# FFN steps behind relu and square in every slot, and result products spread over two slots, in a squared-relu attention and conv-gated FFN kernel

## The chip, the cores and the metric

The kernel runs on one core of a Trainium2 chip. The metric is device time in microseconds (us), the median of several executions. Five engines work side by side, each strictly in the order in which its instructions were written: PE (TensorE, products), DVE (VectorE), ACT (ScalarE), POOL (GpSimd) and SP, which here only issues DMAs. They wait for each other by semaphores.

## The reference

```
scores = (z @ z.T) / S                       # per batch, S = 3136, d_qk = 64
attn   = maximum(scores, 0) ** 2
x      = u * (attn @ v)                      # d_model = 256

h    = maximum(x @ w_in, 0)                  # d_ff = 1024
conv = sum_k conv_w[k] * h shifted by k - 1  # 3 taps along the sequence
out  = (h * sigmoid(conv)) @ w_out
```

There are 4 batches and everything is float32.

## The kernel before

**Tiles.** The sequence is cut into 7 blocks of 448 queries for each batch: 28 blocks, and q is the place of a block in its batch (0 to 6). For one block the keys are 25 tiles of 128 (the last one has 64). One block times one key tile is a *slot*, so there are 700 slots, and the main loop (L582) walks over k, the slot's number. Each float32 operand is held as a high half and a low half, and a product of two of them is three products on PE.

**Attention in a slot.** A *score slot* has two score products (L252, L253) that write a PSUM tile `s`, of which there are two. ACT makes `t`, its relu (L303), DVE multiplies `s` by `t`, the square (L308, `s<-s,t`), ACT copies the high half `ah` (L315), and DVE subtracts for the low half `al` (L121, `al<-s,ah`). Then PE does six products into the block's two sums (L336 to L338, `av`; four at the last tile, L340 and L341). Since the scores are symmetric, a *transposed slot* takes its relu from an earlier block: POOL splits `t` into words (L269), SP sends them to DRAM and fetches them transposed (L281, L289), POOL joins them (L295), and ACT squares them twice, into `s` (L300) and into `ah` (L313). Such a slot has no score products and no L303 and L308, but it still uses a tile `s`, and DVE still makes `al`. Of 25 slots 0, 3, 7, 10, 14, 17, 21 are transposed for q = 0 to 6. With T for a transposed slot and a point for a score slot:

```
q=3  T.T..T.T..T.T..T.T..T.T..
q=4  TT.T.T.TT.T.T.T.TT.T.T.T.
q=5  TTT.TT.TT.TT.TT.TT.TT.TT.
q=6  TTTTTT.TTTTT.TTTTT.TTTTT.
```

**The software pipeline.** In slot k the loop writes the two halves for k+2, relu and square for k+3, the products into `av` for k and the scores for k+4. So the low half `al` of k+2 has to be done before the scores of k+4 can reuse its tile `s`, in the same slot.

**The FFN.** The FFN of a block runs during the next block, in eight parts f of 128 channels. Part f starts in slot s = `FS[f]` of that block (2, 5, 8, 11, 15, 18, 21, 24). Its steps, with the slot in which each stands before the change:

- s: six products into `ph` (`ffn_in`, L369 to L371); there are two tiles `ph`, so part f+2 reuses that of f
- s+1: relu (ACT, L392, `hb`) and first tap (ACT, L401, into `ph`)
- s+2: two more taps (DVE, L406, twice)
- s+3: sigmoid (ACT, L413)
- s+4: gate (DVE, L420); where the running block has q of 0 to 2 it writes a tile `c`, so that `ph` is free then; where q is 3 to 6 it stays in `ph`
- s+5: high half `gh` (ACT, L124); for q of 0 to 2 the low half `gl` on POOL as well
- s+6: for q of 3 to 6 the low half `gl` on DVE (L121, `gl<-ph,gh`), and only then is `ph` free
- s+9: three result products for each of the two halves of the output (`ffn_out`, L437 to L439)

After the last part the result is copied out of PSUM (`evac`, ACT, L459, s+10) and stored (L466, s+12). `gate_x` (L345) and `split_x` (L354) make the FFN's input at the end of a block.

**What sets the order.** The schedule is written by hand. `at(slot, class, function)` puts a step into a list, and in every slot the loop issues: class 0 (PRE), then the halves for k+2, class 1 (MID), relu and square for k+3, class 2 (VEC), class 3 (POST), the transposed tiles' steps, class 4 (PE0), the `av` products and scores, and class 5 (PE1). The constants L34 to L38 give slots and classes of the FFN's steps. A list `need` (L509) sorts the 16 pieces of the FFN's weights by the slot of their first use, and `WS` (L43) gives the n-th of them its place in the first two blocks.

Of the kernel before, what the change touches and what calls it, by code (L numbers as in the profile page):

```python
# [30 lines left out]


FS = [2, 5, 8, 11, 15, 18, 21, 24]
RELU, TAP, ST1, ST2, SIG, GATE, GHI, GLO, OUT0, OUT1 = 1, 1, 2, 2, 3, 4, 5, 6, 9, 9  # L34
EVAC = 10
XS = 1

C_GATE, C_ST, C_G, C_SIG, C_HI, C_LO, C_TAP, C_XS, C_EV, C_V = 0, 1, 1, 1, 1, 0, 3, 3, 0, 5  # L38

QV = 3  # L40

# [16 lines left out]
def kernel(  # L58
# [418 lines left out]
    def at(slot, cls, fn, *args):  # L477
        ev[slot][cls].append((fn, args))


    for q in range(2, QB):
        s = (7 * q) // 2 - LA - 2
# [8 lines left out]
    for b in range(1, B):  # L491
        k0 = (b * QB - 1) * NJ
        for q in range(QB):
            s = k0 - (QB - 2 - q) * NJ + (12 if q % 2 == 0 else 4)
            if q == QB - 2:
                s = k0 + 6
            elif q == QB - 1:
                s = k0 + NJ + 6
# [3 lines left out]
        for j in range(0, NJ, 2):  # L502
            s = k0 + max(last[j] + 2, last.get(j + 1, 0) + 2, V0 + V1 * j // NJ)
# [6 lines left out]
    for i, (_, what, f) in enumerate(sorted(need)):  # L510
        s = WS[i]
# [8 lines left out]
    for blk in range(NBLK - 1):  # L520
        k0 = (blk + 1) * NJ
        at(k0, C_GATE, gate_x, blk, G)
        at(k0 + XS, C_XS, split_x, blk, (G, G))
        for f in range(FC):
            s = k0 + FS[f]
            at(s, POST, ffn_halo, blk, f)
            at(s, PE1, ffn_in, blk, f)
            at(s + RELU, C_TAP, ffn_relu, blk, f)
            at(s + TAP, C_TAP, ffn_tap, blk, f)
            at(s + ST1, C_ST, ffn_conv, blk, f, 1)  # L530
            at(s + ST2, C_ST, ffn_conv, blk, f, 2)
            at(s + SIG, C_SIG, ffn_sig, blk, f)
            lo = V if (blk + 1) % QB >= QV else G
            at(s + GATE, C_G, ffn_gate, blk, f, lo)
            at(s + GHI, C_HI, ffn_hi, blk, f, A)
            at(s + (GLO if lo is V else GHI), C_LO if lo is V else PE1, ffn_lo, blk, f, lo)
            at(s + OUT0, PE0, ffn_out, blk, f, 0)
            at(s + OUT1, PE0, ffn_out, blk, f, 1)
        at(s + EVAC, C_EV, evac, blk)
        at(s + EVAC + 2, POST, store, blk)  # L540

# [107 lines left out]
```

## Time and profile before

| what | value |
|---|---|
| median of 3 runs | 1726.66 us (1726.58 to 1726.93) |
| the profiled execution, its own time | 1727.9 us |
| its span | 1726.1 us |
| PE busy | 1629.6 us (94%), 7656 products |
| DVE busy | 1228.5 us (71%) |
| ACT busy | 1257.5 us (73%) |
| POOL busy | 985.2 us (57%) |
| mean granted clock of PE | 0.992 |
| DMA | 184.58 MB, 107 GB/s on the mean |

PE's ends are modelled, so its busy share is no measure of how near it is to its peak; the distance from one product's start to the next one's is. Start times in the views count from the span's start. In the view by windows the columns are the window, its length, PE's busy time with the number of products, the granted clock, and the DMAs. In the chain of waits they are start, length and instruction, where "issue" is time in which nothing that the profile shows was waited for. In the waits they are who waited for whom, the sum, how often and the longest.

### The profile page before, as it was taken

The numbers are of one execution on the slowest core, as the hardware profiler recorded it, in microseconds if no ns is written. First come the engines' busy times: TensorE is split into PE (matmuls) and PEld (weight loads), VectorE is DVE, ScalarE is ACT, GpSimd is POOL, SyncE is SP. The second block draws the span as 40 slices with busy tenths as digits, with TensorE's granted clock in tenths as the row PEclk, the third lists the DMA queues.
The fourth block names the chain that finished last, engine by engine and source line by source line (L and its number), as shares of the span: only waits on it lengthen the run. The fifth ranks groups of instructions, "written<-read, shape, count | busy, mean of one in ns | idle before, by whom it ended". The sixth has DMA issues, their size and how long they took to land.

```text
span 1726.1 us, 24617 instructions
## 1 busy us (share of the span) xinstructions
PE 1629.6 (94%) x7656; PEld 1429.2 (83%) x7656; DVE 1228.5 (71%) x2080; ACT 1257.5 (73%) x2562; POOL 985.2 (57%) x1345
## 2 busy tenths in 40 slices
PE   6788999999999999999999999999999999999997
PEld 4577888888888888888888888888888888888886
DVE  5788667776777667777767767777776776777766
ACT  5576677778776767778876677777877766777785
POOL 5766655556555665556565565555657555555551
PEclk9899999999999999999999999999999999999999
DMA  5543443457324334445543334454633334344540
GB/s 151 152 116 92 111 102 92 109 118 147 114 76 123 102 89 113 101 107 116 121 137 83 105 104 101 94 114 105 145 94 126 93 82 114 97 100 100 111 97 22
DMA packets 384485, 184.58 MB, mean 107 GB/s; under 512 B 275297, under 2 KB 383329, under 8 KB 384353
## 3 DMA queue, kind: packets, MB, share of 16 engines
q1 hardware_dynamic: 384208, 182.77, 42.9%
q8 instruction: 60, 0.98, 0.3%
q14 instruction: 73, 0.59, 0.1%
q10 hardware_dynamic: 144, 0.23, 0.0%
HBM read 36.59 MB, written 80.28 MB: 68 GB/s over the span
## 4 chain that ended last, share of the span: by engine, by line
PE 47%; ACT 22%; DVE 19%; issue 8%; DMA 1%; POOL 1%; SPq 0%; ACTq 0%; POOLq 0%; DVEq 0%
PE av L336 6%; DVE al L121 6%; PE av L337 6%; PE av L338 6%; ACT ah L315 5%; DVE s L308 5%; PE s L252 5%; DVE ph L406 5%; ACT ph L401 4%; PE ph L371 4%; PE ph L369 4%; ACT hb L392 4%; PE ph L370 4%; PE s L253 3%; PE o L439 3%
## 5 line engine op out<-in xcount | busy, mean ns | idle before, releaser
L121 DVE TENSOR_TENSOR al<-s,ah 128x448 fp32r<-128x448 f32 x672 | 418.2, 622 | 402.1 <-ACT ah L315 243.7
L336 PE MATMUL av<-ah,vl 128*128 128x448 f32 x1344 | 494.9, 368 | 13.6 <-POOL vl L121 8.4
L337 PE MATMUL av<-ah,vh 128*128 128x448 f32 x1344 | 494.3, 368 | 0.0
L338 PE MATMUL av<-al,vh 128*128 128x448 f32 x1344 | 493.1, 367 | 0.0
L315 ACT CAST ah<-s 128x448 fp32r<-128x448 f32 x412 | 219.5, 533 | 272.1 <-DVE s L308 271.5
L295 POOL COPY tj<-tp 128x896 uint16<-128x896 uint16 x288 | 351.5, 1225 | 0.3
L406 DVE SCALAR_TENSOR_TENSOR ph<-hb,cw,ph 128x448 f32<-128x448 f32 (+1 forms) x448 | 306.6, 685 | 12.2 <-ACT ph L401 4.4
L269 POOL COPY pl<-t 128x896 uint16<-128x896 uint16 x312 | 291.8, 943 | 16.2 <-DMA dq<-pl 13.8
L308 DVE TENSOR_TENSOR s<-s,t 128x448 f32<-128x448 f32 x412 | 258.1, 626 | 49.7 <-ACT t L303 49.4
L394 POOL COPY halo<-hb 128x2 f32<-128x2 f32 x192 | 35.8, 187 | 451.1 <-ACT hb L392 451.1
L336 PEld LDWEIGHTS av<-ah,vl 128*128 128x128 f32 x1344 | 254.3, 189 | 39.4 <-POOL vl L121 11.0
L337 PEld LDWEIGHTS av<-ah,vh 128*128 128x128 f32 x1344 | 254.3, 189 | 20.6
L338 PEld LDWEIGHTS av<-al,vh 128*128 128x128 f32 x1344 | 254.0, 189 | 20.8
L303 ACT ACTIVATE t<-s 128x448 f32<-128x448 f32 x412 | 224.4, 545 | 33.1 <-POOL pl L269 16.2
L252 PE MATMUL s<-zq,zhh 128*128 128x448 f32 x412 | 176.4, 428 | 72.9 <-DVE al L121 62.6
L252 PEld LDWEIGHTS s<-zq,zhh 128*128 128x128 f32 x412 | 78.4, 190 | 155.3 <-DVE al L121 140.2
L369 PE MATMUL ph<-xh,wih 128*128 128x448 f32 x448 | 165.2, 369 | 4.9 <-DVE gl L121 4.9
L413 ACT ACTIVATE ph<-ph 128x448 f32<-128x448 f32 (+1 forms) x224 | 119.7, 534 | 67.0 <-DVE ph L406 66.3
L437 PE MATMUL o<-gh,wol 128*128 128x448 f32 (+1 forms) x448 | 164.4, 367 | 0.6 <-ACT gh L124 0.6
L371 PE MATMUL ph<-xl,wih 128*128 128x448 f32 x448 | 164.8, 368 | 0.0
L370 PE MATMUL ph<-xh,wil 128*128 128x448 f32 x448 | 164.7, 368 | 0.0
L439 PE MATMUL o<-gl,woh 128*128 128x448 f32 (+1 forms) x448 | 163.9, 366 | 0.8 <-POOL gl L121 0.8
(78 smaller groups left out, 2515.9 us busy)
## 6 DMA issues: line engine op xcount, KB each, us to landing
dq<-pl SPq DMA_DIRECT2D x252, 224.0 KB, 2.4
ut<-in_u_dram SPq DMA_DIRECT2D x28, 448.0 KB, 4.1
vst<-in_v_dram SPq DMA_DIRECT2D x48, 256.0 KB, 3.0
dq<-pl SPq DMA_DIRECT2D x84, 112.0 KB, 2.4
out_dram<-ob SPq DMA_DIRECT2D x20, 448.0 KB, 3.7
zt<-in_z_dram SPq DMA_DIRECT2D x28, 224.0 KB, 3.2
tp<-dq SPq DMA_TRANSPOSE x288, 3.3
wr<-in_moe_w_in_dram SPq DMA_DIRECT2D x8, 256.0 KB, 3.5
```

Source lines behind the costliest of these rows:

```text
L121: eng.tensor_tensor(out=out, in0=a, in1=b.bitcast(F32), op=ALU.subtract)
L252: nc.tensor.matmul(s[:, :NB], lhsT=zhh[:, w], rhs=zq[blk], start=True, stop=False)
L269: nc.gpsimd.tensor_copy(pl[k], rl.pop(k).bitcast(U16).rearrange("p (n h) -> p h n", h=2))
L295: nc.gpsimd.tensor_copy(tj[k].bitcast(U16).rearrange("p (n h) -> p h n", h=2), t)
L308: nc.vector.tensor_tensor(out=s, in0=s, in1=rl[k], op=ALU.mult)
L315: nc.scalar.copy(ah[k], sc[k][:, :NB])
L336: nc.tensor.matmul(o, lhsT=vl[:, j, d], rhs=h, start=first, stop=False)
L337: nc.tensor.matmul(o, lhsT=vh[:, j, d], rhs=h, start=False, stop=False)
L338: nc.tensor.matmul(o, lhsT=vh[:, j, d], rhs=l, start=False, stop=False)
L369: nc.tensor.matmul(o, lhsT=wih[:, dc, w], rhs=xh[blk][:, dc], start=(dc == 0), stop=False)
L371: nc.tensor.matmul(o, lhsT=wih[:, dc, w], rhs=xl[blk][:, dc], start=False, stop=(dc == DC - 1))
L406: nc.vector.scalar_tensor_tensor(out=c, in0=hb[blk, f][:, k : e + k], scalar=cw[:, f, k : k + 1], in1=c, op0=ALU.mult, op1=ALU.add,)
```

## The change

Only constants change, and `C_ST` is split in two:

```diff
-RELU, TAP, ST1, ST2, SIG, GATE, GHI, GLO, OUT0, OUT1 = 1, 1, 2, 2, 3, 4, 5, 6, 9, 9
-EVAC = 10
+RELU, TAP, ST1, ST2, SIG, GATE, GHI, GLO, OUT0, OUT1 = 1, 1, 2, 2, 3, 4, 5, 6, 10, 11
+EVAC = 12
 XS = 1
 
-C_GATE, C_ST, C_G, C_SIG, C_HI, C_LO, C_TAP, C_XS, C_EV, C_V = 0, 1, 1, 1, 1, 0, 3, 3, 0, 5
+C_GATE, C_ST1, C_ST2, C_G, C_SIG, C_HI, C_LO = 0, 2, 2, 2, 3, 3, 2
+C_TAP, C_XS, C_EV, C_V = 3, 3, 3, 5
...
-            at(s + ST1, C_ST, ffn_conv, blk, f, 1)
-            at(s + ST2, C_ST, ffn_conv, blk, f, 2)
+            at(s + ST1, C_ST1, ffn_conv, blk, f, 1)
+            at(s + ST2, C_ST2, ffn_conv, blk, f, 2)
```

On DVE the taps and the gate go from between the low half and the square (class 1) to behind the square (class 2), and `gl` from the slot's start (class 0) to behind the square. On ACT the sigmoid and `gh` go from between `ah` and relu (class 1) to behind relu (class 3), and the copy `evac` from the slot's start to class 3. On PE a part's result products stood together at s+9, and now the first half stands at s+10 and the second at s+11, so that of three slots one has the `ffn_in` products, one the first and one the second half (for the parts in slots 15, 18 and 21 the first half falls into the slot of the `ffn_in` products). `evac` and the store move by two slots. POOL's `gl` stays at its place, though its input `gh` is written later in the slot. `need` sorts a little differently, so that from the fourth piece on `w_in` pieces come sooner and `w_out` pieces later, at the same places. The number of instructions is the same. The last block's own FFN has constants of its own and is not touched. In the changed kernel every line number is higher by one.

On ACT, in a block with q = 0, these are the rows of its slots 8, 9 and 10 before the change (`t` is relu, `zhh` and `vh` prepare the next batch, `gh` stands in slot 10):

```order
L315 CAST ah<-s 128x448
L413 ACTIVATE ph<-ph 128x450
L303 ACTIVATE t<-s 128x448
L315 CAST ah<-s 128x448
L303 ACTIVATE t<-s 128x448
L137 CAST zhh<-zt 128x448
L392 ACTIVATE hb<-ph 128x448
L401 ACTIVATE ph<-hb,cw 128x450
L124 CAST vh<-vst 128x512
L315 CAST ah<-s 128x448
L124 CAST gh<-c 128x450
L303 ACTIVATE t<-s 128x448
```

And these are the same three slots with the change:

```order
L316 CAST ah<-s 128x448
L304 ACTIVATE t<-s 128x448
L414 ACTIVATE ph<-ph 128x450
L316 CAST ah<-s 128x448
L304 ACTIVATE t<-s 128x448
L138 CAST zhh<-zt 128x448
L393 ACTIVATE hb<-ph 128x448
L402 ACTIVATE ph<-hb,cw 128x450
L125 CAST vh<-vst 128x512
L316 CAST ah<-s 128x448
L304 ACTIVATE t<-s 128x448
L125 CAST gh<-c 128x450
```

The sigmoid (`ph<-ph`) and `gh` have changed places with the `t` behind them. On DVE, in a block with q = 0, slots 6 to 8 before the change (`s<-s,t` is the square, L406 the taps, L420 the gate):

```order
L121 TENSOR_TENSOR al<-s,ah 128x448
L420 TENSOR_TENSOR c<-ph,hb 128x450
L308 TENSOR_TENSOR s<-s,t 128x448
L121 TENSOR_TENSOR al<-s,ah 128x448
L406 SCALAR_TENSOR_TENSOR ph<-hb,cw,ph 128x450 x2
L308 TENSOR_TENSOR s<-s,t 128x448
L121 TENSOR_TENSOR al<-s,ah 128x448
L308 TENSOR_TENSOR s<-s,t 128x448
```

With the change:

```order
L122 TENSOR_TENSOR al<-s,ah 128x448
L309 TENSOR_TENSOR s<-s,t 128x448
L421 TENSOR_TENSOR c<-ph,hb 128x450
L122 TENSOR_TENSOR al<-s,ah 128x448
L309 TENSOR_TENSOR s<-s,t 128x448
L407 SCALAR_TENSOR_TENSOR ph<-hb,cw,ph 128x450 x2
L122 TENSOR_TENSOR al<-s,ah 128x448
L309 TENSOR_TENSOR s<-s,t 128x448
```

Low half and square now follow each other, and the FFN's step comes third. On DVE, in a block with q = 3, slots 10 and 11 before the change, where slot 11 has the `ffn_in` products of a part on PE and `gl` of the part two before it on DVE:

```order
L121 TENSOR_TENSOR al<-s,ah 128x448
L406 SCALAR_TENSOR_TENSOR ph<-hb,cw,ph 128x448 x2
L308 TENSOR_TENSOR s<-s,t 128x448
L121 TENSOR_TENSOR gl<-ph,gh 128x448
L121 TENSOR_TENSOR al<-s,ah 128x448
L308 TENSOR_TENSOR s<-s,t 128x448
```

With the change:

```order
L122 TENSOR_TENSOR al<-s,ah 128x448
L309 TENSOR_TENSOR s<-s,t 128x448
L407 SCALAR_TENSOR_TENSOR ph<-hb,cw,ph 128x448 x2
L122 TENSOR_TENSOR al<-s,ah 128x448
L309 TENSOR_TENSOR s<-s,t 128x448
L122 TENSOR_TENSOR gl<-ph,gh 128x448
```

`gl`, which frees the tile `ph`, was first in its slot and is now third.

## The prediction

> **What bounds the kernel now.** First I ask how far PE is from its own pace. The timeline gives a stretch without stalls: its first and last product, with 33 steps between them, and the one behind them.
>
> ```profile
> 475.88 0.36 PE L369 MATMUL ph<-xh,wih 128*128 128x448 f32 x1
> ...
> 482.58 0.36 PE L338 MATMUL av<-al,vh 128*128 128x448 f32 x1
> 482.88 0.47 PE L252 MATMUL s<-zq,zhh 128*128 128x448 f32 x1
> ```
>
> (482.58 - 475.88) / 33 = 0.203 us for a product, and a product that had to wait comes 0.1 us later still (0.30 instead of 0.20), as its weight load isn't hidden. Next, the windows, cut at the ends of blocks 1 and 2, of blocks 7 to 13 (one batch, q = 0 to 6) and of the last batch as a whole (the one between fills 859.3 to 1275.7).
>
> ```profile
> 82.90:149.80 66.90, 58.54 (x266) 0.97 0.42 117
> 149.80:214.80 65.00, 59.84 (x279) 0.97 0.37 94
> 442.40:507.80 65.40, 62.66 (x293) 1.00 0.38 117
> 507.80:570.90 63.10, 60.93 (x289) 1.00 0.36 102
> 570.90:631.10 60.20, 58.38 (x280) 1.00 0.36 98
> 631.10:692.10 61.00, 57.38 (x276) 1.00 0.42 104
> 692.10:749.10 57.00, 55.44 (x266) 1.00 0.48 104
> 749.10:803.80 54.70, 54.26 (x261) 1.00 0.50 106
> 803.80:859.30 55.50, 54.23 (x260) 1.00 0.58 127
> 1275.70:1689.30 413.60, 401.05 (x1911) 1.00 0.41 101
> ```
>
> Length minus products times 0.203 is what PE loses. For q = 0 to 6: 5.9, 4.4, 3.4, 5.0, 3.0, 1.7, 2.7 us, together 26 of 417. The batches behind take 416.4 (859.3 to 1275.7) and 413.6 us, so this repeats. A block is thus within 3 to 9% of PE's pace, and no reordering can win more than that. Who makes PE wait, and what do ACT and DVE wait for? From the waits:
>
> ```profile
> ACT ah L315 <- DVE s L308: 271.5, 244, 3.1
> PE s L252 <- DVE al L121: 62.6, 109, 3.7
> DVE s L308 <- ACT t L303: 49.4, 115, 1.8
> PE ph L369 <- DVE gl L121: 4.9, 5, 3.7
> ```
>
> PE waits for `al`, which frees the tile `s` for the scores. ACT waits for the square far more than PE waits for anything. Why, the chain of waits shows for one part of the FFN in the block with q = 0, from its `ffn_in` products to the next part's relu:
>
> ```profile
> 451.75 0.20 PE ph L369
> ...
> 452.76 0.21 PE ph L371
> 453.00 0.55 ACT hb L392
> 453.64 0.64 ACT ph L401
> 454.28 0.36 ACT vh L124
> 454.64 0.08 issue
> 454.72 0.54 ACT ah L315
> 455.28 0.62 DVE al L121
> 455.90 0.61 DVE ph L406
> 456.57 0.56 issue
> 457.14 0.63 DVE s L308
> 457.82 0.41 issue
> 458.22 0.54 ACT ph L413
> 458.76 0.47 ACT t L303
> 459.26 0.64 DVE s L308
> 459.95 0.41 issue
> 460.35 0.55 ACT t L303
> 460.90 0.45 ACT zhh L137
> 461.35 0.46 ACT hb L392
> ```
>
> From 453.00 to 461.35 the chain never passes through PE: 8.35 us of ACT and DVE by turns (the "issue" at 457.82 is the `ah` that the square released). PE's share of three score slots is 36 products, 7.31 us. **In these blocks the ping-pong of ACT and DVE is the bound, not PE.** Three FFN steps stand in it only because of their place: the taps ahead of the square (455.90 to 457.14, 1.24 us), and the sigmoid ahead of relu (458.22 to 458.76, 0.54 us); elsewhere the gate and `evac`.
>
> **The change part by part.** *Taps and gate behind the square, sigmoid, `gh` and `evac` behind relu.* No instruction is added, so the price is only where they stand. In the new order a part's chain from its first relu (hb) runs: to `al` 453.00 to 455.28 less the 0.44 of `vh` and issue, which not every part has: 1.84 us. Then square and taps. DVE's steps without a wait follow at 0.53 us, as two rows of its timeline show:
>
> ```profile
> 652.87 0.62 DVE L121 TENSOR_TENSOR gl<-ph,gh 128x448 fp32r<-128x448 f32 x1
> 653.40 0.61 DVE L121 TENSOR_TENSOR al<-s,ah 128x448 fp32r<-128x448 f32 x1
> ```
>
> So `al` to square 0.53, square to taps 0.53, taps 1.24, the next `al` 0.62 and 0.06 until PE: 4.82 us after hb the scores of slot s+7 are free. PE reaches them 28 products and a step after its last `ffn_in` product, 29 x 0.203 = 5.89, and hb starts 0.24 after that product (452.76 to 453.00): at 5.65. If the square has to wait for PE's scores instead, these start 10 steps after the last `ffn_in` product, relu 0.44 later (0.20 for the second product and the 0.24), the square 0.57 behind it, that is 2.80 after hb in place of 2.37, and the tile is free at 5.25. Both come before 5.65, and with a `vh` (0.44) still before or beside it: **in blocks with q of 0 to 2 PE becomes the bound.** What covers the taps is the `ah` of the next slot and PE's slack of 0.4 us; without it they cost what exceeds it. I leave 0.8 us a block for `queries`, `xh`, `evac` and the 0.1 us of exposed weight loads (it lies between nothing and the 1.7 us that the best block loses now). Won: q = 0 to 2, 5.9 + 4.4 + 3.4 - 2.4 = 11.3 us in each of three batches, 33.9. Blocks 1 and 2 of the first batch lose 12.9 and 8.4 us, much of it to preparing weights, which stays; I count only what their like win later, 3.6 + 2.6 = 6.2, with 0 and 21 as ends.
>
> *`gl` behind the square, for q of 3 to 6.* Here a wait grows. The `ffn_in` products of part f+2 need `ph`, which `gl` of part f frees, in the same slot, in six of eight parts (part 2's and 3's `gl` come a slot earlier than the products). Before, `gl` ran while DVE waited for `ah` anyway, and only 5 products waited for it. Now it stands behind `al` and square. Queued behind the waiting product are the next slot's `av` products and scores, and hb on ACT. The path from one `ffn_in` to the next, all by the rows above: hb to `al` 1.84, `al` to taps 0.53, taps 1.24, `al` to `gl` 0.53, `gl` 0.62, release and exposed weight load 0.17, six products and hb 1.25 (451.75 to 453.00): 6.18 us, and 0.53 for each square that stands in it, so 6.71 with one and 7.24 with two. Against it stand the products of these three slots. For q = 3: slot 8, one square, 32 products (6.50): 0.21 short; slots 11 and 21, two squares, 34 products (6.90): 0.34 each; slot 24, one square, 27 products (5.48): 1.23. Together 2.1. In the same way q = 4 gets 0.21, 0.21, 0.70, q = 5 0.21, 1.10, q = 6 twice 0.09, 0.21, 0.95; 5.9 us a batch in all. With 0.8 us a block for the rest as above, 12.4 (now) - 5.9 - 3.2 = 3.3 us are won in each of four batches, 13.2. The ends are no such wait at all (+23.6) and the rival below.
>
> *The result products in two slots.* The same 48 a block, now 14, 11 and 11 products in three slots and not 20, 8 and 8. They are in the counts above; by itself it wins nothing where PE is the bound. Its operands are ready four slots earlier (`gl` at s+6 at the latest). `evac` now has one slot, not two, until the next block's first result product overwrites `o`: relu and two copies, three ACT steps of at most 0.64 (the rows above), against the 14 products of slot 11, 2.84 us. It costs nothing. The store and transposes on SP's queue move by a slot or two, far ahead of a use. In POOL's queue `gl` waits about 0.5 us longer for `gh`, and the words for DRAM behind it; POOL was 57% busy, so nothing, and at worst the same 0.5 us for the 88 of them in 11 blocks, were each to reach PE, 44 (in the second rival).
>
> *Weights and the two ends.* The 16 pieces keep their places, and their steps end slots ahead of use: 0, between -3 and +3 us (the lost time of blocks 1 and 2 has such steps). Block 0 has no FFN. Behind the last block one or two slots' worth of result products and `evac` come later among the 36.8 us that the span (1726.1) goes on after 1689.3, with another FFN in them: 0, between -1 and +1.5.
>
> Sum: 33.9 + 6.2 + 13.2 = 53 us, off the profiled execution's 1727.9 (span 1726.1 and 1.8 around it): 1674.6. The runs' median lies 1.2 below it: **1673 us**.
>
> [...] DVE's square waited 115 times for relu, 49.4 us, so what stands behind a square waits as well. [...] That is the third rival's mechanism; if all 49.4 us fell on PE the sum would be nearly nil.
>
> **The rivals.** *PE alone is left.* Neither `gl` nor the rest makes it wait: 53 + 23.6 + the 0.8 of some 25 blocks, half of it, 10: 1640 to 1655. For it: `gl`'s shortfalls are tenths. Against: slot 24 lacks 0.7 us or more in every one of these blocks.
>
> *The wait for `gl` is three times as dear.* Some 94 `ffn_in` groups at 0.45 us, 42 instead of 23.6 us, and stalls of POOL's queue beside it: 1690 to 1712. For it: the estimate is made of steady paths, and each stall delays hb and the chain behind it.
>
> *Slower.* One mechanism: `gl` stands behind a square that itself waits for relu, so that `ffn_in` begins only after `al`, square and `gl`: 0.53 + 0.53 + 0.62 + 0.17 less the two score products' 0.41, 1.44 us; say 1.0 us for 94 groups, 94 us in place of 23.6: 1673 + 70 = 1743. It decides from (53 + 23.6) / 94 = 0.8 us a group. [...] Against: transposed slots have no square, and they are 10 to 21 of 25 in exactly these blocks.
>
> *Nothing happens*, because ACT's waits were never PE's: 1722 to 1730. Against it stands the chain, which for 8.35 us doesn't touch PE.
>
> **How the numbers follow.** Forecast (1655 to 1695) 0.62; PE alone 0.10; dearer `gl` 0.14; slower 0.08; nothing 0.06, of which 0.04 is within 0.2% (3.5 us, about what a measurement of this kernel can tell from no change). Faster: 0.62 + 0.10 + 0.14 + 0.02 = 0.88. The range 1650 to 1706 leaves out the last two cases, a third of the first rival and a sixth of the second, 0.2 in all.
>
> **What would show it.** Right: ACT's wait for the square falls from 271.5 us to under 100; the windows with q = 0 come to 60 to 61 us; PE's wait for `al` falls by more than half; a wait of `ffn_in` for `gl` appears, 15 to 35 us, most at slot 24. Wrong: q = 0 still over 63 us (the chain then has something that I haven't seen), or windows with q of 3 to 6 longer than now (`gl`), or new waits of L252 or L437 for POOL.

## The result, and the profile after

The changed kernel takes 1699.38 us (median of 4 runs, 1699.05 to 1699.81), beside 1726.62 us of the kernel before on the same chip: ratio 0.9846, 95% interval 0.9829 to 0.9863. That is 27 us won; 53 were forecast. The time lies in the range, the direction is right, and half of the gain is missing. The profiled span went from 1726.1 to 1697.7 us at the same mean granted clock, 0.992.

From the page of the changed kernel, busy time by engine and the chain's shares (before, on the kernel's page, the chain was `PE 47%`, `ACT 22%`, `DVE 19%`):

```profile
PE 1615.3 (95%) x7656; PEld 1433.9 (84%) x7656; DVE 1215.1 (72%) x2080; ACT 1277.1 (75%) x2562; POOL 982.5 (58%) x1345
...
PE 72%; DVE 13%; issue 6%; ACT 6%; POOL 1%; DMA 1%; SPq 0%; POOLq 0%; DVEq 0%; ACTq 0%
```

The same products and about the same busy time on ACT and DVE (before 1257.5 and 1228.5 us), but the chain now runs through PE for 72% of the span. DVE's 13% is what is left to explain. The waits of the changed kernel (who waited for whom, sum in us, times, longest):

```profile
ACT ah L316 <- DVE s L309: 97.0, 215, 2.5
DVE s L309 <- ACT t L304: 77.2, 177, 2.2
PE s L253 <- DVE al L122: 31.0, 33, 2.6
PE ph L370 <- DVE gl L122: 26.0, 35, 3.1
```

ACT's wait for the square fell by 174.5 us and PE's idle time until `al` by half. The wait of `ffn_in` for `gl`, once 4.9 us in 5 places, grew to 26.0 in 35. The weight loads of the same line (PEld) show it in 59 places, the 35 among them:

```profile
PEld ph L370 <- DVE gl L122: 47.2, 59, 3.4
```

Idle times rest on modelled ends, so from here on I count *lost starts*: the distance from one product's start to the next, less 0.203 us, wherever it is over 0.24. By the line of the late product that gives, over the whole trace: before `ffn_in` 8.2 us before the change and 46.4 after it (5.9 and 5.1 of them in the last block's own FFN, which the change doesn't touch), before the scores 126.1 and 61.3, in all 160.5 and 131.0. Next, the windows of the same blocks as in the prediction, 1 and 2 and then q = 0 to 6 (window, length, PE busy with its products, granted clock, DMA share, GB/s). Each begins behind the last `av` product of the block before, so it also holds the scores and `ffn_in` of that block's slot 24:

```profile
82.90:145.70 62.80, 57.66 (x259) 0.94 0.44 119
145.70:207.00 61.30, 57.99 (x280) 1.00 0.39 105
435.60:498.10 62.50, 60.59 (x293) 1.00 0.42 127
498.10:558.20 60.10, 59.34 (x290) 1.00 0.37 104
558.20:616.00 57.80, 57.50 (x279) 1.00 0.40 105
616.00:676.80 60.80, 57.40 (x276) 1.00 0.41 103
676.80:734.90 58.10, 55.47 (x265) 1.00 0.48 102
734.90:789.40 54.50, 53.84 (x262) 1.00 0.51 108
789.40:844.40 55.00, 53.95 (x260) 1.00 0.56 124
```

Length less products times 0.203: blocks 1 and 2 lose 10.2 and 4.5 us, q = 0 to 6 lose 3.0, 1.2, 1.2, 4.8, 4.3, 1.3 and 2.2. Against the kernel before, q = 0 to 2 won 8.3 us a batch, blocks 1 and 2 won 6.6, and **q = 3 to 6, which were to win 3.3, lost 0.2**. Lost starts, put to the slot in which each product stands and added up over the whole trace, say it more sharply: 28.3 us won in q = 0 to 2, 6.8 in blocks 1 and 2, and 7.6 lost in q = 3 to 6. The largest part of the miss lies there. One of its places, at the end of slot 7 and in slot 8 of the block with q = 3 (timeline: start, length, instruction, and in brackets the idle time before it and what ended it):

```profile
637.28 0.36 PE L254 MATMUL s<-zq,zll 128*128 128x448 f32 x1
...
637.68 0.55 ACT L304 ACTIVATE t<-s 128x448 f32<-128x448 f32 x1 [0.94 <-PE s L254]
...
638.26 0.63 DVE L309 TENSOR_TENSOR s<-s,t 128x448 f32<-128x448 f32 x1 [0.39 <-ACT t L304]
...
638.50 0.37 PE L339 MATMUL av<-al,vh 128*128 128x448 f32 x1
...
638.80 0.61 DVE L122 TENSOR_TENSOR gl<-ph,gh 128x448 fp32r<-128x448 f32 x1
...
639.47 0.47 PE L370 MATMUL ph<-xh,wih 128*128 128x448 f32 x1 [0.61 <-DVE gl L122]
```

PE's last score product, relu, square, `gl`, and back to PE: 637.28 to 639.47, 2.19 us. PE had seven steps to do in it (the last score product and six of `av`), 1.42 us. `gl` had all its inputs 2.5 us before (`gh` was done at 636.27); it waited only because it is behind a square that waits for relu. The prediction's path to `ffn_in` entered only at `hb`. This second entrance isn't in it.

This place is an example, not the rule. In blocks 1 to 27, 73 groups of `ffn_in` start late, by 41.3 us together. Followed back from `gl` by what released each step, 24 of them (16.2 us) go back to PE's scores, relu and square: 8 as here (7.0 us, slot 8 with q = 3 and 4), 16 with the two taps and an `al` between that square and `gl`. 39 (21.0 us) go back to `hb` and the `ffn_in` products ahead of it, the prediction's own path; 9 (3.5 us) to an `al` that waited for products of `av`; one in block 1 (0.6 us) waited for no `gl` on DVE.

### The profile page after: what moved, and what is told of

It reads as the page before. It is cut to its first block, busy times and chain, and to the rows that moved or that the text cites. A ratio compares the mean times of both kernels' runs of the same rounds, so it can differ in the third digit from the quotient of the medians.

```text
span 1697.7 us, 24837 instructions
## 1 busy us (share of the span) xinstructions
PE 1615.3 (95%) x7656; PEld 1433.9 (84%) x7656; DVE 1215.1 (72%) x2080; ACT 1277.1 (75%) x2562; POOL 982.5 (58%) x1345
## 4 chain that ended last, share of the span: by engine, by line
PE 72%; DVE 13%; issue 6%; ACT 6%; POOL 1%; DMA 1%; SPq 0%; POOLq 0%; DVEq 0%; ACTq 0%
PE av L337 11%; PE av L338 11%; PE av L339 11%; PE ph L370 6%; PE ph L372 5%; PE ph L371 5%; PE s L253 5%; PE o L440 4%; PE o L438 4%; PE o L439 4%; PE s L254 4%; DVE al L122 3%; DVE s L309 3%; DVE ph L407 3%; ACT t L304 2%
## 5 line engine op out<-in xcount | busy, mean ns | idle before, releaser
L337 PE MATMUL av<-ah,vl 128*128 128x448 f32 x1344 | 496.0, 369 | 10.2 <-POOL vl L122 7.8
L309 DVE TENSOR_TENSOR s<-s,t 128x448 f32<-128x448 f32 x412 | 258.7, 628 | 78.2 <-ACT t L304 77.2
L338 PEld LDWEIGHTS av<-ah,vh 128*128 128x128 f32 x1344 | 254.8, 190 | 20.4
L393 ACT ACTIVATE hb<-ph 128x448 f32<-128x448 f32 x224 | 122.6, 547 | 118.8 <-PE ph L372 117.2
L253 PE MATMUL s<-zq,zhh 128*128 128x448 f32 x412 | 163.6, 397 | 39.8 <-DVE al L122 31.0
L370 PE MATMUL ph<-xh,wih 128*128 128x448 f32 x448 | 171.9, 384 | 28.1 <-DVE gl L122 26.0
L314 ACT ACTIVATE ah<-tj 128x448 fp32r<-128x448 f32 x288 | 165.1, 573 | 0.0
```

Of the source, the lines that this page charges most:

```text
L309: nc.vector.tensor_tensor(out=s, in0=s, in1=rl[k], op=ALU.mult)
L337: nc.tensor.matmul(o, lhsT=vl[:, j, d], rhs=h, start=first, stop=False)
L338: nc.tensor.matmul(o, lhsT=vh[:, j, d], rhs=h, start=False, stop=False)
L370: nc.tensor.matmul(o, lhsT=wih[:, dc, w], rhs=xh[blk][:, dc], start=(dc == 0), stop=False)
```

## The experiments

Two suspects: what `gl` inherits from the square, and the spread, which was priced at nothing although the products in question could cover exactly that path. Medians, ratios to the runs of the kernel before that stood beside each, with 95% intervals, and lost starts in us. The medians of the kernel before in these groups of runs lie between 1725.8 and 1728.6 us, so the difference of two kernels from different groups is good to about 3 us.

| kernel | us | ratio | lost before `ffn_in` | before scores | all |
|---|---|---|---|---|---|
| before | 1726.6 | 1 | 8.2 | 126.1 | 160.5 |
| the change | 1699.4 | 0.9846 (0.9829 to 0.9863) | 46.4 | 61.3 | 131.0 |
| order_only | 1674.8 | 0.9699 (0.9683 to 0.9715) | 32.9 | 51.7 | 106.0 |
| spread_only | 1726.0 | 0.9997 (0.9988 to 1.0007) | 12.0 | 114.0 | 158.6 |
| out_9_10 | 1689.4 | 0.9775 (0.9759 to 0.9792) | 40.9 | 56.7 | 120.5 |
| gl_mid | 1677.0 | 0.9714 (0.9699 to 0.9728) | 24.3 | 59.7 | 108.7 |
| gl_first | 1686.4 | 0.9759 (0.9745 to 0.9774) | 11.5 | 82.6 | 120.3 |
| gl_only | 1762.8 | 1.0212 (1.0197 to 1.0227) | 65.1 | 103.7 | 195.8 |
| taps_back | 1724.2 | 0.9981 (0.9971 to 0.9990) | 48.7 | 88.8 | 156.1 |
| ctile | 1665.0 | 0.9636 (0.9621 to 0.9650) | 5.1 | 65.7 | 97.5 |
| ctile_before | 1742.4 | 1.0093 (1.0078 to 1.0108) | 3.1 | 141.9 | 174.8 |
| ctile_together | 1649.2 | 0.9556 (0.9540 to 0.9571) | 4.3 | 51.5 | 79.7 |
| mid_together | 1659.4 | 0.9604 (0.9590 to 0.9619) | 14.1 | 54.6 | 90.9 |
| first_together | 1670.1 | 0.9665 (0.9651 to 0.9679) | 6.7 | 72.3 | 103.5 |
| ctile_9_10 | 1657.2 | 0.9595 (0.9578 to 0.9612) | 3.6 | 59.2 | 90.0 |
| ctile_10_10 | 1707.0 | 0.9887 (0.9870 to 0.9905) | 5.0 | 111.5 | 139.9 |

### The two halves of the change apart

`order_only` has the new order and keeps the result products together at s+9 (its edit stands against the changed kernel):

```diff
-RELU, TAP, ST1, ST2, SIG, GATE, GHI, GLO, OUT0, OUT1 = 1, 1, 2, 2, 3, 4, 5, 6, 10, 11
-EVAC = 12
+RELU, TAP, ST1, ST2, SIG, GATE, GHI, GLO, OUT0, OUT1 = 1, 1, 2, 2, 3, 4, 5, 6, 9, 9
+EVAC = 10
```

> The new order within a slot, but the result products together at s+9 as before. Theory 1, with the refinement that the square ahead of gl waits for scores that PE itself made one slot earlier, so that only the products between those scores and ffn_in cover gl: six result products more stand there, 1.2 us, and the wait of ffn_in for gl falls from 45 to under 15 us; 1670 to 1690 us, faster than the change. As I put it in the prediction (the spread by itself wins nothing): within 5 us of 1699. Theory 2: 1700 to 1712 us, since 20, 8 and 8 products fit the other engines worse.

`spread_only` is the kernel before with the result products spread:

```diff
-RELU, TAP, ST1, ST2, SIG, GATE, GHI, GLO, OUT0, OUT1 = 1, 1, 2, 2, 3, 4, 5, 6, 9, 9
-EVAC = 10
+RELU, TAP, ST1, ST2, SIG, GATE, GHI, GLO, OUT0, OUT1 = 1, 1, 2, 2, 3, 4, 5, 6, 10, 11
+EVAC = 12
```

> The kernel before with only the result products spread (s+10, s+11, evac at s+12); the order within a slot is the old one. By both theories the ping-pong of ACT and DVE stays the bound for q of 0 to 2 and gl stays first: 1720 to 1735 us, a difference of at most 0.5% from the kernel before.

The order alone wins 52 us; the spread on the old order changes nothing. Together they win 27, so **on the new order the spread costs 25 us**: 13 more lost before `ffn_in` (32.9 to 46.4) and 10 more before the scores (51.7 to 61.3). The latter is all in slot 24, which has no result product with the spread and six without it: it loses 16.1 us in place of 3.6, the other slots 45.2 in place of 48.2. The time of `order_only` lay in the expected range, but not for the expected reason alone: the wait at `ffn_in` was to fall under 15 us and stayed at 33. The windows of `order_only`, for the same nine blocks:

```profile
82.40:145.70 63.30, 57.36 (x266) 0.98 0.44 122
145.70:205.30 59.60, 57.42 (x280) 1.00 0.41 105
429.50:491.40 61.90, 61.12 (x294) 1.00 0.41 123
491.40:550.30 58.90, 58.84 (x290) 1.00 0.38 109
550.30:607.60 57.30, 57.18 (x280) 1.00 0.40 104
607.60:665.90 58.30, 57.19 (x276) 1.00 0.43 108
665.90:721.90 56.00, 54.81 (x266) 1.00 0.49 106
721.90:776.40 54.50, 53.89 (x262) 1.00 0.51 108
776.40:831.60 55.20, 54.35 (x260) 1.00 0.57 126
```

By the same reckoning q = 0 to 6 lose 2.2, 0.0, 0.5, 2.3, 2.0, 1.3 and 2.4 us here. With the spread it is 0.8, 1.2 and 0.7 us more in q = 0 to 2, and 2.5 and 2.3 more in q = 3 and 4. Slot 8 with q = 3, in the timeline of `order_only`:

```profile
626.71 0.36 PE L254 MATMUL s<-zq,zll 128*128 128x448 f32 x1
626.91 0.37 PE L438 MATMUL o<-gh,wol 128*128 128x448 f32 x1
...
627.58 0.62 DVE L122 TENSOR_TENSOR al<-s,ah 128x448 fp32r<-128x448 f32 x1
...
628.11 0.62 DVE L309 TENSOR_TENSOR s<-s,t 128x448 f32<-128x448 f32 x1
...
628.64 0.61 DVE L122 TENSOR_TENSOR gl<-ph,gh 128x448 fp32r<-128x448 f32 x1
...
629.14 0.36 PE L339 MATMUL av<-al,vh 128*128 128x448 f32 x1
...
629.34 0.44 PE L370 MATMUL ph<-xh,wih 128*128 128x448 f32 x1
```

From the last score product to the end of `gl` the path is even longer than in the change (626.71 to 629.25, 2.54 us; there 637.28 to 639.41, 2.13), since an `al` comes ahead of the square. But PE now has six result products to do first, 13 steps, 2.63 us, and `ffn_in` starts 0.20 us behind the last `av`. In the change these six stand at slots 9 and 10 and cover nothing here.

### How much cover

`out_9_10`, against the changed kernel, has the first half at s+9 and the second at s+10:

```diff
-RELU, TAP, ST1, ST2, SIG, GATE, GHI, GLO, OUT0, OUT1 = 1, 1, 2, 2, 3, 4, 5, 6, 10, 11
-EVAC = 12
+RELU, TAP, ST1, ST2, SIG, GATE, GHI, GLO, OUT0, OUT1 = 1, 1, 2, 2, 3, 4, 5, 6, 9, 10
+EVAC = 11
```

> The changed kernel with the result products one slot earlier (s+9 and s+10, evac at s+11), so that three of them stand between the scores that the square ahead of gl needs and the ffn_in products that wait for gl. Theory 1 (those products cover the path scores, relu, square, gl): the wait lies between that of the change (no result products there) and of order_only (six): 1682 to 1692 us, and lost starts before L370 and L371 of 36 to 43 us (45 and 32 in the other two). Theory 2 (what costs is that they are spread over two slots): within 5 us of 1699.

In the change three of the eight slots with `ffn_in` (15, 18, 21) also hold three result products, in `out_9_10` all eight hold three, in `order_only` five (2, 5, 8, 11, 24) hold six: 9, 24 and 30 products a block. The lost starts before `ffn_in` are 46.4, 40.9 and 32.9 us, and the times 1699.4, 1689.4 and 1674.8, in `out_9_10` as expected. The time moves more than this one wait, so the scores take part.

### `gl` at other places in its slot

Class 1 is between `al` and the square (`gl_mid`, whose edit of the changed kernel this is), class 0 the slot's start, as before the change (`gl_first`, with 0 in the same place).

```diff
-C_GATE, C_ST1, C_ST2, C_G, C_SIG, C_HI, C_LO = 0, 2, 2, 2, 3, 3, 2
+C_GATE, C_ST1, C_ST2, C_G, C_SIG, C_HI, C_LO = 0, 2, 2, 2, 3, 3, 1
```

> The changed kernel with gl between al and the square (class 1 in place of 2), the result products spread as in the change. If the wait of ffn_in for gl comes from the square ahead of gl, which itself waits for relu and so for PE's scores of the slot before (theory 1), it falls from 45 us of lost starts before L370 and L371 to under 15, and al is held up less than with gl ahead of it: 1665 to 1682 us. If gl is late only because it stands behind al at all (theory 2), the wait stays over 30 us and the time within 8 us of 1699.

> The changed kernel with gl back at the start of its slot, ahead of al. Theory 1: the wait for gl goes, al in these slots comes up to 0.53 us later in about 94 slots, a third of which reach PE: 1665 to 1680 us. Theory 2: 1690 us or more, the wait for al grows by what the wait for gl loses.

`gl_only` is the kernel before with this step alone of the change:

```diff
-C_GATE, C_ST, C_G, C_SIG, C_HI, C_LO, C_TAP, C_XS, C_EV, C_V = 0, 1, 1, 1, 1, 0, 3, 3, 0, 5
+C_GATE, C_ST, C_G, C_SIG, C_HI, C_LO, C_TAP, C_XS, C_EV, C_V = 0, 1, 1, 1, 1, 2, 3, 3, 0, 5
```

> The kernel before with gl alone moved behind the square (class 2), all else old: result products together at s+9, taps and gate ahead of the square. Theory 1: the six result products cover a part of the path, and the taps no longer share the slot, so 12 to 30 us more than before, 1738 to 1757 us, all of it in windows with q of 3 to 6. If gl is hidden anyway there: within 4 us of 1727.

One place earlier, ahead of the square only, halves the wait (46.4 to 24.3) and takes 22 us off the time: so about half of it is what `gl` gets from standing behind the square. That is the square's own 0.53 us on DVE as well as its wait for relu: in the change the square right ahead of `gl` had waited for relu in 8 of the 73 late groups only, those with 7.0 us. The time lies in the range of theory 1; the rest of the wait, which it put under 15 us, stays. At the slot's start the wait all but goes (11.5), but then `gl` delays `al`, and the scores lose 21 us more (61.3 to 82.6); the time came between the ranges of the two theories. Neither place is free. On the old order the step alone makes the kernel 37 us *slower* than the kernel before beside it, dearer than expected; there the square right ahead of `gl` had waited for relu in 41 of 78 late groups, with 48.0 us lost. In the waits of `gl_only`:

```profile
PE s L252 <- DVE al L121: 46.3, 87, 2.4
PE ph L369 <- DVE gl L121: 42.7, 47, 3.6
```

So this step of the change costs, and the rest pays for it.

### The taps alone ahead of the square again

The changed kernel, `taps_back` with its one edit:

```diff
-C_GATE, C_ST1, C_ST2, C_G, C_SIG, C_HI, C_LO = 0, 2, 2, 2, 3, 3, 2
+C_GATE, C_ST1, C_ST2, C_G, C_SIG, C_HI, C_LO = 0, 1, 1, 2, 3, 3, 2
```

> The changed kernel with the two taps alone put back ahead of the square. If the taps are the main part of the ping-pong of ACT and DVE (1.24 us a part in the chain of before), the windows with q of 0 to 2 lose much of what the change won there (8.3 us a batch): they get 1 to 2.5 us longer each, and with q of 3 to 6 the path to gl gets no longer where the square comes later: 1704 to 1722 us. If the sigmoid's and gate's places are what counts: within 5 us of 1699.

25 us slower than the change, a little more than expected: without the taps' new place the rest of the change is worth 2 to 4 us. 19.0 us more are lost in q = 0 to 2, 2.1 a block, as expected, and 6.4 more in q = 3 to 6, which was not. In the waits and, for the block with q = 0, on the timeline of `taps_back`:

```profile
ACT ah L316 <- DVE s L309: 181.3, 228, 2.1
...
PE s L253 <- DVE al L122: 54.2, 86, 2.6
```

```profile
441.88 0.55 ACT L304 ACTIVATE t<-s 128x448 f32<-128x448 f32 x1
441.91 0.62 DVE L122 TENSOR_TENSOR al<-s,ah 128x448 fp32r<-128x448 f32 x1 [1.71 <-ACT ah L316]
...
442.45 1.40 DVE L407 SCALAR_TENSOR_TENSOR ph<-hb,cw,ph 128x448 f32<-128x448 f32 x2
...
443.76 0.63 DVE L309 TENSOR_TENSOR s<-s,t 128x448 f32<-128x448 f32 x1
```

Relu is done at 442.43, and the square waits for the two taps until 443.76. This is the prediction's main mechanism, and it is shown: ACT's wait for the square comes back (97.0 to 181.3) and PE's for `al` with it.

### The wait for `gl` taken out: the tile `c` for every block

If the gate writes a tile `c` also for q of 3 to 6, `ph` is free at the gate and `ffn_in` doesn't wait for `gl`. `ctile` has this edit on the changed kernel, `ctile_before` the same on the kernel before.

```diff
-        if lo is nc.gpsimd:
+        if lo is nc.gpsimd or blk < NBLK - 1:
             cc[blk, f] = o = wk.tile([P, NB + 2], F32, tag="c", name="c", bufs=2)[:, :e]
```

> The changed kernel, but the gate writes a tile c in all blocks (so far only where q is 0 to 2), and gh and gl read that. So ph is free at the gate, two slots earlier, and ffn_in cannot wait for gl; gl itself stays behind the square. Theory 1 (the shortfall of the prediction is the wait of ffn_in for gl, some 45 us by the gaps between PE's products): nearly all of it comes back, 1655 to 1668 us, and the windows with q of 3 to 6 each lose less than 2 us against PE's pace. Theory 2 (in these blocks ACT and DVE are late anyway, and the wait for gl is only where it shows): PE waits for al in its place, 1685 to 1700 us.

> Control: the kernel before with the c tile in all blocks. gl was first in its slot, and only 5 products waited for it (4.9 us), so the tile by itself is worth little by either theory: 1718 to 1729 us. If the tile wins much more than that, ctile's gain is not that of the wait for gl.

The wait is gone (46.4 to 5.1) and the time falls by 34 us to 1665.0, within the expected range. (The blocks with q = 4 were to lose under 2 us and lose 3.1 by lost starts, half of it before the scores of slot 18.) On the kernel before the same edit was to win a little or nothing and *cost* 16 us. There `gl` stands at the slot's start, ahead of `al`, and it takes longer itself (838 ns on the mean, not 616; more on that at the end); the scores lose 142 us in place of 126. That the delay of `al` is the way from the one to the other is argued, not isolated.

### What the spread still costs without that wait

`ctile_together` is `ctile` with the edit below; `ctile_9_10` has 9, 10 and 11 there, `ctile_10_10` 10, 10 and 11.

```diff
-RELU, TAP, ST1, ST2, SIG, GATE, GHI, GLO, OUT0, OUT1 = 1, 1, 2, 2, 3, 4, 5, 6, 10, 11
-EVAC = 12
+RELU, TAP, ST1, ST2, SIG, GATE, GHI, GLO, OUT0, OUT1 = 1, 1, 2, 2, 3, 4, 5, 6, 9, 9
+EVAC = 10
```

> The new order in a slot, the c tile in all blocks, and the result products together at s+9. With ffn_in free of gl, theory 1 says that the spread neither costs nor wins much (the block losses for q of 0 to 2 add up to 3.4 us a batch together and 4.0 spread): 1655 to 1668 us, within 6 us of ctile (1665). If the spread itself costs, whatever gl does (theory 2): 1640 to 1650 us.

> ctile (no wait for gl) with the result products one slot earlier, at s+9 and s+10, still spread. Theory A (what the spread costs beside gl is that no result product stands in slots 23 and 24, where PE comes early to the scores and waits for al; ctile loses 11 us in slot 24 of blocks 7 to 26, ctile_together 1.5): slot 24 now has three, so its loss falls to 3 to 7 us and the time to 1653 to 1660 us. Theory B (20, 8 and 8 suits ACT and DVE better than 14, 11, 11, wherever they stand): 1662 to 1668 us.

> ctile with all six result products of a part together, but at s+10, so again none in slots 23 and 24. Theory A: the loss in slot 24 stays near 11 us, 1660 to 1670 us. Theory B (together is better than spread): 1645 to 1655 us.

With the wait for `gl` gone, the products together at s+9 still win 16 us (1665.0 to 1649.2): the theory that the spread harms only through `gl` is refuted. `ctile_together` is the fastest kernel here, 77 us ahead of the kernel before and 50 ahead of the change; its waits and its chain:

```profile
PE s L253 <- DVE al L122: 21.5, 36, 2.6
```

```profile
PE 78%; ACT 9%; DVE 5%; issue 3%; POOL 3%; DMA 1%; SPq 0%; POOLq 0%; ACTq 0%; DVEq 0%
```

Is it being together, or the place? `ctile_10_10` has them together one slot later and is 58 us slower than `ctile_together`, outside both theories' ranges. So it is the place. In blocks 7 to 26 the scores lose 17.0 us with the products at 9 and 9, 20.4 at 9 and 10, 27.3 at 10 and 11, and 63.7 at 10 and 10. By their places, most of the eight parts have in that order 6, 3, 3 and 0 of these products on PE in slot s+2, where the taps are behind the square, or at the start of s+3, ahead of the scores that wait for the `al` behind those taps. Apart from slot 24 they lose 15.6, 12.8, 16.1 and 49.3 us: with none of these products much is lost, and three are as good as six. This is worked out from the order and was not isolated. Between 9 and 9, 9 and 10, and 10 and 11 the difference is mostly slot 24's. One of the two theories had put the whole gain on slot 24, which has four `av` products in place of six: there `ctile` loses 11.2 of its 27.3 us, `ctile_9_10`, with three result products in that slot, 7.6 (its time is as that theory had it), and `ctile_together`, with six, 1.5. `ctile_10_10`, which loses 12.5 and 10.1 us at slots 2 and 11 as well as 14.4 at slot 24, shows that it isn't the whole.

`mid_together` and `first_together` are `gl_mid` and `gl_first` with the edit of `order_only`.

> The new order, result products together at s+9, and gl between al and the square; no c tile, so gl keeps an operand in PSUM. Theory 1: both remedies add up, the wait for gl all but goes (lost starts before L370 and L371 under 8 us): 1640 to 1655 us, no slower than ctile_together (1649). If gl ahead of the square holds up the square, and so al of the next slot, more than it saves: 1660 to 1675 us.

> The new order, result products together, gl first in its slot as in the kernel before: all of the change that concerns taps, gate, sigmoid, gh and evac, and nothing else. Theory 1: al comes 0.53 us later in some slots, as in gl_first (1686 spread), less the 16 to 25 us that the spread costs: 1655 to 1672 us.

1659.4 and 1670.1: `mid_together` lies between its two ranges, with 14.1 us still lost before `ffn_in`, `first_together` in its own. Against `gl_mid` and `gl_first` the place of the result products is worth 18 and 16 us. With three ways to treat `gl` it is thus 16 to 18 us, and 25 where `gl` is behind the square.

## Why the prediction was half right

The measured gains beside the forecast's terms (us), once by the windows, each batch's figure times three or four as there, and once by lost starts, each put to its own slot and added up over the whole trace:

| term | forecast | order_only, windows | the change, windows | order_only, lost starts | the change, lost starts |
|---|---|---|---|---|---|
| q = 0 to 2 | 33.9 | 33.0 | 24.9 | 34.9 | 28.3 |
| q = 3 to 6 | 13.2 | 17.6 | -0.8 | 9.1 | -7.6 |
| blocks 1 and 2 | 6.2 | 9.2 | 6.6 | 10.1 | 6.8 |
| block 0 and the end | 0 | | | 0.5 | 2.0 |
| sum | 53.3 | 59.8 | 30.7 | 54.6 | 29.5 |
| the span fell by | | 54.3 | 28.4 | 54.3 | 28.4 |

The lost starts add up to the fall of the span within 1.1 us, so they are the better account; the windows count the scores and `ffn_in` of slot 24 to the next block. That `order_only` meets the sum so well is in part luck: 4.1 us too little in q = 3 to 6 and 3.9 too much in blocks 1 and 2 cancel.

- **Taps, gate and sigmoid out of the ping-pong: right.** `taps_back` shows that the taps carry it, and `order_only` wins 33.0 us in q = 0 to 2 where 33.9 were forecast. ACT's wait for the square fell under 100 (97.0), and PE's idle time until `al` by half, 62.6 to 31.0, where "more than half" was named. Without the spread it is 20.1. The windows with q = 0 were to come to 60 to 61 us; they are 62.5, and 61.9 without the spread. The window with q = 4 became longer, 58.1 after 57.0, which the prediction had named as a sign of being wrong.
- **The step that failed is the price of the result products in two slots: "by itself it wins nothing", "It costs nothing".** On the old order that holds (`spread_only`). On the order that the same diff makes it costs 25 us. I counted products between one `ffn_in` and the next. That count changes only ahead of slot 24 (27 in place of 30, 0.6 us a block, which the forecast booked under the wait for `gl`), and I looked for any other cost at `o`, `evac` and POOL. What counts is which products PE still has to do while a path through ACT and DVE runs, and where that path begins.
- **The wait for `gl` was priced too low**, 23.6 us against 41.3 in blocks 1 to 27. One reason is the entrance by scores, relu and square, which the path from `hb` leaves out. In the batch read (blocks 10 to 14) q = 3 was to lack 0.21 at slot 8 and loses 0.88, 0.34 at slots 11 and 21 and loses 1.03 at each, and q = 4 was to lack 0.21 at slot 8 and loses 0.88. Slots 2 and 5 of the next q = 0 were to lack nothing and lose 0.68 and 0.66: their `ph` is freed by `gl` of the last two parts of the FFN before, in the same way.
- **The path from `hb` was also read 0.16 us too short.** The rows of a product in the chain of waits begin at the modelled end of the one before; on the timeline of the kernel before the first `ffn_in` product starts at 451.59, not 451.75, the last at 452.60, not 452.76, and `hb` comes 0.40 us behind it, not 0.24. So PE reaches the scores of slot s+7 at 5.49 after `hb`, not 5.65; the two paths of the prediction, at 4.82 and 5.25, still come before. With these 0.16 us slots 24 of q = 3, 21 of q = 4 and 5, and 24 of q = 5 come to 1.39, 0.37, 0.37 and 1.26, and lose 1.37, 0.37, 0.41 and 1.30. Slot 24 of q = 4 and 6 was priced too high (0.70 and 0.95; it loses 0.11 and 0.65).
- **The exposed weight load** of 0.1 us was read off the wrong row: 482.58 to 482.88 is a wait for `al`. It shows one product later, at 483.19, 0.31 behind the one that waited: its load (PEld, 0.19 us) starts at 482.99, 0.11 after the product that waited, where on pace a load starts together with the product before its own (both at 482.18). Over the trace of the kernel before, the product behind one that came more than 0.4 us after its predecessor follows 0.31 us later on the median of 167.
- **The rivals.** The second, `gl` three times as dear, gave the time (1690 to 1712) and about the price (42 us in 94 groups; measured 41.3 in 73) but named as the cause that the paths aren't steady, and nothing of the spread. The third's mechanism, which I had priced at 1.0 us a group and called unlikely since transposed slots have no square, does act, in the change on a smaller scale: right ahead of `gl` in 8 groups (7.0 us), a slot earlier in 16 more (9.2 us). The row behind it grew: DVE's square waits 77.2 us for relu, not 49.4. In the traces of both kernels the instructions of each engine all start in the order in which they were written (2080 on DVE), and what that order costs shows in `gl_mid`: moved ahead of the square alone, `gl` stands behind neither the square's own time nor its wait, and 22 us come back.
- **Weights, block 0 and the end**, put at nothing, show no cost: block 0 still ends at 82.9, and 36.3 us come after the start of the last `av` product of the last block, before 37.1. The new order of the weights' pieces, which begins with the sixth piece and not the fourth, was not isolated.

Still open: why the spread costs nothing on the old order was not traced, and whether a kernel with `c` everywhere and result products in yet other slots beats 1649.2 us was not tried.

## What to carry to other kernels

When a step is put behind an instruction on an engine that works in order, as DVE did here (its 2080 instructions all start in the written order), follow every entrance into the path through it, not only the one that its own inputs come by: the moved step now stands behind that instruction's own time and behind whatever it waits for. Work on the bounding engine that waits for nothing is cover for such paths, so moving it is priced by which path it stands beside in the *new* order; the same move cost 0 us on the old order and 25 on the new. Two edits of one diff are best measured apart: here one won 52 us and the other gave half of it back.

## What the runs showed of the hardware

In `ctile_before`, where both inputs of DVE's `gl` are in SBUF (`c` and `gh`), it took 838 ns on the mean, against 616 in the kernel before with one in PSUM (`ph`), and it was longer only where POOL worked beside it. (With `ph` none of the 132 in the kernel before takes over 627 ns, though POOL works for at least 0.6 us beside 57 of them.) Groups by form of the kernel before (line, engine, operation, count, then busy time and mean ns):

```profile
L121 DVE TENSOR_TENSOR gl<-ph,gh 128x448 fp32r<-128x448 f32 x128 | 78.8, 616 | 0.6 <-ACT gh L124 0.6
```

and of `ctile_before`:

```profile
L121 DVE TENSOR_TENSOR gl<-c,gh 128x448 fp32r<-128x448 f32 x128 | 107.3, 838 | 0.6 <-ACT gh L124 0.6
```

Two of them on the timeline of `ctile_before`, one with POOL idle, one beside a copy on POOL:

```profile
782.72 0.62 DVE L121 TENSOR_TENSOR gl<-c,gh 128x448 fp32r<-128x448 f32 x1
...
788.92 1.21 POOL L295 COPY tj<-tp 128x896 uint16<-128x896 uint16 x1
...
789.48 1.07 DVE L121 TENSOR_TENSOR gl<-c,gh 128x448 fp32r<-128x448 f32 x1
```

Over the trace of `ctile_before`, the 45 that no POOL instruction overlaps take 617 ns on the mean, the 64 with at least 0.6 us of overlap 1005. For the 39 that begin beside a POOL instruction, and see no other begin, the length went by when POOL was done: all end 0.41 to 0.49 us after it, whether 0.18 or 0.85 us of it were left. Why `gl` takes longer there was not shown. In `ctile` `gl` is as slow (828 ns on the mean), but there it stands behind the square, and `ffn_in` no longer waits for it.
